# Moving the load slots of a streaming decode kernel to a multiple of 512 bytes in SBUF

## The chip, the cores and the metric

The kernel runs on one core of a Trainium2 chip. The metric is device time in microseconds (us), the median of several executions. Nearly all effects are under 2%, so kernels are compared with runs of the kernel before that were taken in the same call on the same chip.

The profile calls the engines PE (TensorE; PEld are its weight loads), DVE (VectorE), ACT (ScalarE), POOL (GpSimd) and SP (SyncE, which issues the loads). A packet is what the profile records as one item of a transfer: here the contiguous bytes that go into one partition.

## The reference, cut to what matters

One token goes through a transformer block with adaptive layer norm: conditioning, attention over a long cache, and a gated feed-forward.

```python
mod = silu(c) @ w_mod                        # 1024 x 6144
h = layernorm(x) * (1 + ca) + sa
q = h @ wq                                   # 1024 x 4096, 32 heads, 4 KV groups
scores = q . k_cache * 128 ** -0.5           # k_cache 4 x 65536 x 128, bf16
o = softmax(scores) . v_cache                # v_cache the same size
x = x + ga * (o @ wo)
h = layernorm(x) * (1 + cb) + sb
x = x + gb * ((gelu(h @ w_gate) * (h @ w_up)) @ w_down)
```

Everything is read once: 185.6 MB, of which the two caches are 134.2 MB. There is almost no reuse, so the time is first of all the time of reading.

## The kernel before

All large inputs arrive through ten slots of 8,192 bf16 elements (16 KB) in each of the 128 partitions, which are slices of one tensor. A K load fills two slots (32 KB per partition), a V load one; the weights use one slot each, wholly or in part. SP issues the loads in a fixed order, each as soon as the slots that it overwrites are free.

```python
SLOT = 8192
NSLOT = 10

ident = sb("ident", [P, P], dt.bfloat16)
identf = sb("identf", [P, P])
# ... some forty further tensors, in order ...
t_dn = sb("t_dn", [P, KD])
y_col = sb("y_col", [P, KD])
y_row = sb("y_row", [KD, P], dt.bfloat16)
# ... PSUM ...
slot_all = nc.alloc_sbuf_tensor("slots", [P, NSLOT * SLOT], dt.bfloat16)
slots = [slot_all[:, i * SLOT:(i + 1) * SLOT] for i in range(NSLOT)]

def issue_ready():
    while issued[0] < len(loads):
        j = loads[issued[0]]
        if any(q.freed is None for q in j.prev):
            return
        SP.wait(*(q.freed for q in j.prev))
        sp.dma_start(j.view, j.src).then_inc(j.tok[0], 16)
        issued[0] += 1

kh = [A_k_cache[0, g].rearrange("(p n) d -> p n d", p=P) for g in range(Hkv)]   # vh alike
# chunk i: 64 rows of 128 elements per partition, which lie together in HBM
j_k[i] = plan_load(kv_src(kh, i, KU), flat(KU * CH, DH), ...)     # KU = 2 chunks, 32 KB a partition
j_v[j] = plan_load(kv_src(vh, j), flat(CH, DH), ...)              # 1 chunk, 16 KB a partition
```

In the built program tensors lie in the order of their allocation, each rounded up to 32 bytes. The slots start at byte 65,088 of each partition, which is 127 x 512 + 64. Since a slot is 16 KB, all ten slots start 64 bytes past a multiple of 512. Every run of the large inputs in HBM starts at a multiple of 2 KB within its tensor.

## Time and profile before

| what | value |
|---|---|
| time, median of 3 runs | 443.07 us |
| span of the profiled run | 442.0 us |
| data moved, mean rate | 185.89 MB, 421 GB/s |
| time of the load queue's packets, share of 16 engines' span | 98.7% |
| TensorE (PE) busy | 351.4 us (80%) |

The profile's page of the kernel before; the first line under the heading is the engines' busy time, the line under the third heading is the load queue (packets, megabytes, time of its packets as a share of the 16 DMA engines' span), and the fourth heading is the chain of work that ended last:

```profile
span 442.0 us, 15336 instructions
## 1 busy us (share of the span) xinstructions
PE 351.4 (80%) x7107; PEld 316.9 (72%) x7107; DVE 176.2 (40%) x300; ACT 146.5 (33%) x553; POOL 11.7 (3%) x25
...
q1 hardware_dynamic: 11632, 185.61, 98.7%
...
DMA 62%; PE 33%; issue 1%; DVE 1%; SPq 1%; ACT 1%
```

The load queue's own packets fill 98.7% of the time of all 16 DMA engines. No compute engine is above 80%. The chain that ended last is mostly DMA.

The table by stretches of the same kernel (bounds in us, length, then busy time of each engine with its number of instructions, granted clock, DMA share, GB/s):

```profile
60.00:100.00 40.00, 34.97 (x706) 34.46 (x707) 16.14 (x19) 10.65 (x35) 0.00 (x0) 0.68 1.01 429
100.00:200.00 100.00, 90.62 (x2029) 88.58 (x2025) 49.85 (x78) 44.78 (x171) 0.00 (x0) 0.80 1.00 428
200.00:300.00 100.00, 89.63 (x1966) 87.46 (x1963) 48.61 (x78) 45.08 (x171) 0.00 (x0) 0.80 1.01 430
300.00:380.00 80.00, 73.26 (x1589) 71.75 (x1586) 38.45 (x58) 36.99 (x149) 0.00 (x0) 0.76 1.01 430
```

The last two numbers are what to read: the DMA share is 1.00 or 1.01 everywhere, so the transfers never run dry in the attention stage, and the rate stays at 428 to 430 GB/s.

The timeline of the last microseconds (start us, length us, engine, line, what; in brackets the idle time before it and what ended it):

```profile
436.66 2.94 PE L372 MATMUL b<-u_col,slots 128*128 128x1 bf16 x96 [3.07 <-DMA slots<-in_B_w_down_dram]
...
440.47 0.28 DVE L850 CAST y_row<-b 8x128 bf16<-8x128 f32 x1 [0.47 <-PE b L848]
```

The last group of products starts when one of the last loads lands. The very last load lands while this group runs, at 439.18 us by the landings in the trace, and eight products start on it. The chain that ended last shows this (start us, length us, what):

```profile
414.74 24.44 DMA slots<-in_B_w_down_dram
439.23 0.39 PE b L372 x8
440.47 0.28 DVE y_row L850
```

After the last landing the kernel needs about 1.6 us to its last result. So the time is: start of the stream + duration of the stream + a fixed end.

### The profile page before, as it was taken

Reading aid. Unit: us, or ns where it says so; the run is one execution under the profiler, and the core shown is the slowest. Engines: PE = TensorE matmul, PEld = TensorE weight load, DVE = VectorE, ACT = ScalarE, POOL = GpSimd, SP = SyncE. Lnnn points to the kernel's source line nnn. Section 1 sums busy time; section 2 is a strip of 40 time slices with the busy share of each in tenths; the row PEclk is TensorE's granted clock in tenths of the full one; section 3 lists DMA queues with packets and bytes.
Section 4 is the critical chain, followed back from the end, with each engine's and each line's share of the span. In section 5 each row is a group of like instructions: output and inputs, shape, how many; then the busy total and the mean of one; then the engine's idle time right before and its main releaser. Section 6 shows DMA issues by size and latency. Waiting matters only on the chain.

```text
span 442.0 us, 15336 instructions
## 1 busy us (share of the span) xinstructions
PE 351.4 (80%) x7107; PEld 316.9 (72%) x7107; DVE 176.2 (40%) x300; ACT 146.5 (33%) x553; POOL 11.7 (3%) x25
## 2 busy tenths in 40 slices
PE   0557449997889989998989879898998989547644
PEld 0214139987889989997989879798988979533234
DVE  4102013545534544554445544454446445242100
ACT  1000001334524643343535534344554433500000
POOL 8100000000000000000000000000000000000000
PEclk9955555969956975967778986877768686658955
DMA  8999999999999999999999999999999999999995
GB/s 330 430 427 425 443 434 414 423 442 417 428 446 414 442 412 442 416 439 430 423 440 420 435 421 437 439 418 446 412 443 414 440 420 431 424 429 418 427 419 211
DMA packets 11957, 185.89 MB, mean 421 GB/s; under 512 B 1568, under 2 KB 1568, under 8 KB 1952
## 3 DMA queue, kind: packets, MB, share of 16 engines
q1 hardware_dynamic: 11632, 185.61, 98.7%
q8 instruction: 13, 0.21, 0.2%
q10 hardware_dynamic: 304, 0.01, 0.0%
q14 instruction: 8, 0.07, 0.0%
HBM read 185.60 MB, written 0.00 MB: 420 GB/s over the span
## 4 chain that ended last, share of the span: by engine, by line
DMA 62%; PE 33%; issue 1%; DVE 1%; SPq 1%; ACT 1%
DMA slots<-in_A_v_cache_dram 39%; PE kt_ps L561 18%; DMA slots<-in_A_k_cache_dram 10%; PE b L625 7%; PE sc_ps L581 6%; DMA slots<-in_B_w_down_dram 6%; DMA slots<-in_B_w_up_dram 4%; DMA slots<-in_w_mod_dram 4%; PE b L605 1%; SPq L234 1%; PE kt_ps L392 1%; ACT p_sb L691 1%; PE b L595 1%; DVE kt_sb L751 0%; PE b L760 0%
## 5 line engine op out<-in xcount | busy, mean ns | idle before, releaser
L561 PE MATMUL kt_ps<-ident,slots 128*128 128x128 bf16 x2048 | 178.0, 257 | 11.0 <-DMA slots<-in_A_k_cache_dram 10.0
L561 PEld LDWEIGHTS kt_ps<-ident,slots 128*128 128x128 bf16 x2048 | 153.8, 117 | 12.8 <-issue 8.7
L660 DVE COPY kt_sb<-kt_ps 128x2048 bf16<-128x2048 bf16 x96 | 117.6, 1225 | 111.7 <-PE kt_ps L561 111.6
L660 ACT ACTIVATE kt_sb<-kt_ps 128x2048 bf16<-128x2048 bf16 x32 | 60.1, 1877 | 185.1 <-PE kt_ps L561 185.1
L625 PE MATMUL b<-p_sb,slots 128*128 128x8 bf16 x2176 | 75.7, 167 | 25.0 <-DMA slots<-in_A_v_cache_dram 16.1
L625 PEld LDWEIGHTS b<-p_sb,slots 128*128 128x128 bf16 x2176 | 69.5, 100 | 27.9 <-DMA slots<-in_A_v_cache_dram 17.3
L691 ACT ACTIVATE p_sb<-sc_ps,mneg 128x64 bf16<-128x64 f32 x256 | 83.6, 560 | 4.9 <-DVE mneg L686 4.9
L691 ACT ACTIVATION_READ_ACCUMULATOR p_sb<-sc_ps,mneg 128x1 f32 x256 | 77.2, 364 | 0.0
L581 PE MATMUL sc_ps<-q_buf,kt_sb 128*128 128x8 bf16 x2112 | 69.8, 167 | 0.9 <-issue 0.9
L581 PEld LDWEIGHTS sc_ps<-q_buf,kt_sb 128*128 128x128 bf16 x2112 | 67.6, 100 | 1.0 <-issue 1.0
L392 PE MATMUL kt_ps<-slots,h_pad 128*32 128x512 bf16 x176 | 17.5, 526 | 13.1 <-DMA slots<-in_A_wq_dram 6.4
L679 DVE TENSOR_REDUCE m_col<-sc_ps 128x8 f32<-128x512 f32 x32 | 21.8, 682 | 5.1 <-PE sc_ps L581 5.1
L684 DVE TENSOR_REDUCE mg<-b 8x1 f32<-8x128 f32 x32 | 8.9, 279 | 35.2 <-PE b L595 35.2
L392 PEld LDWEIGHTS kt_ps<-slots,h_pad 128*32 128x32 bf16 x176 | 5.3, 117 | 23.0 <-DMA slots<-in_A_wq_dram 8.3
L392 PE MATMUL kt_ps<-slots,s_pad 128*32 128x512 bf16 x96 | 13.6, 588 | 8.7 <-DMA slots<-in_w_mod_dram 8.7
L392 PEld LDWEIGHTS kt_ps<-slots,s_pad 128*32 128x32 bf16 x96 | 3.8, 123 | 17.6 <-DMA slots<-in_w_mod_dram 12.5
L605 PE MATMUL b<-negi,mg 8*128 8x8 f32 x66 | 15.6, 306 | 0.0
L605 PEld LDWEIGHTS b<-negi,mg 8*128 8x128 f32 x66 | 12.5, 235 | 2.1
L453 PEld LDWEIGHTS sc_ps<-identf,kt_sb 128*128 128x128 f32 (+1 forms) x48 | 7.6, 204 | 8.2 <-DVE kt_sb L774 4.3
L686 DVE COPY mneg<-b 128x8 f32<-128x8 f32 x32 | 5.3, 167 | 19.6 <-PE b L605 19.6
L453 PE MATMUL sc_ps<-identf,kt_sb 128*128 128x128 f32 (+1 forms) x48 | 9.1, 352 | 4.5 <-DVE kt_sb L774 2.4
L372 PE MATMUL b<-u_col,slots 128*128 128x1 bf16 x224 | 6.6, 165 | 6.8 <-DMA slots<-in_B_w_down_dram 6.7
(97 smaller groups left out, 84.9 us busy)
## 6 DMA issues: line engine op xcount, KB each, us to landing
slots<-in_A_k_cache_dram SPq DMA_DIRECT2D x16, 4096.0 KB, 20.7
slots<-in_A_v_cache_dram SPq DMA_DIRECT2D x32, 2048.0 KB, 27.3
slots<-in_w_mod_dram SPq DMA_DIRECT2D x8, 1536.0 KB, 17.9
slots<-in_A_wq_dram SPq DMA_DIRECT2D x4, 2048.0 KB, 35.7
slots<-in_A_wo_dram SPq DMA_DIRECT2D x4, 2048.0 KB, 32.8
slots<-in_B_w_gate_dram SPq DMA_DIRECT2D x4, 1792.0 KB, 21.0
slots<-in_B_w_up_dram SPq DMA_DIRECT2D x4, 1792.0 KB, 22.8
slots<-in_B_w_down_dram SPq DMA_DIRECT2D x3, 2048.0 KB, 27.7
```

Of the source, the lines that this page charges most:

```text
L372: ins = pe.matmul(bank[:, j:j + 1], view[:, kk, j * P:(j + 1) * P], rhs[:, k0 + kk:k0 + kk + 1], start=first, stop=True, skip_group_check= ...
L392: ins = pe.matmul(out, pad[:, k, :], jb.view[:, kk, c0:c0 + ROW], start=k <= last_k[0], stop=k >= last_k[1], skip_group_check=True,)
L453: ins = pe.transpose(dst[:, i * w:i * w + n], src[:, a], identf[0:src.shape[0], 0:n])
L561: ins = pe.transpose(kt_ps[:, half * 2048 + t * P:half * 2048 + (t + 1) * P], j_k[i - i % KU].view[:, i % KU * CH + b * TB + t, :], ident[ ...
L581: ins = pe.matmul(sc_ps[:, base + n * REP:base + (n + 1) * REP], kt_sb[:, j % 2, n, :], q_buf[:, j % SITES, :], start=True, stop=True,)
L605: ins = pe.matmul(b6[:, 256:256 + REP], mg8[:, j % 2:j % 2 + 1].to_broadcast([REP, P]), negi[:, :], start=True, stop=True,)
L625: ins = pe.matmul(b7[:, s * REP:(s + 1) * REP], j_v[j].view[:, n, :], p_sb[:, s, n, :], start=(n == 0), stop=(n == CH - 1),)
L660: ev[i % SITES][b].done(act.activation(dst, src, ACT.Copy) if E_ is AC else dve.tensor_copy(dst, src))
L679: m1[s].done(dve.tensor_reduce(m_col[:, j % 2, :].unsqueeze(2), scv, AX.X, ALU.max))
L684: m2[s].done(dve.tensor_reduce(mg8[:, j % 2:j % 2 + 1], b6[0:REP, 32:32 + P], AX.X, ALU.max))
L686: v_mc[j] = DVE.done(dve.tensor_copy(mneg[:, j, :], b6[:, 256:256 + REP]))
L691: ins = act.activation(p_sb[:, s, :, h], scv[:, h, :], ACT.Exp, bias=mneg[:, j, h:h + 1], scale=scale, accum_out=z_all[:, j, h:h + 1],)
```

## The change

The intent is to let every packet that a load writes start on a round SBUF address. Four 32-byte tensors are allocated earlier and the slots directly behind them, so that the slots start at byte 16,896 = 33 x 512.

```diff
     ident = sb("ident", [P, P], dt.bfloat16)
+    x_col = sb("x_col", [P, KD])
+    x_nat = sb("x_nat", [P, KD])
+    sg_col = sb("sg_col", [P, KD])
+    th_col = sb("th_col", [P, KD])
+    slot_all = nc.alloc_sbuf_tensor("slots", [P, NSLOT * SLOT], dt.bfloat16)
     identf = sb("identf", [P, P])
     ...
-    x_col = sb("x_col", [P, KD])
-    x_nat = sb("x_nat", [P, KD])
-    sg_col = sb("sg_col", [P, KD])
-    th_col = sb("th_col", [P, KD])
     ...
-    slot_all = nc.alloc_sbuf_tensor("slots", [P, NSLOT * SLOT], dt.bfloat16)
```

No instruction is added, removed or reordered. Only the tensors' addresses differ. The two big working tensors (the transposed K and the probabilities) keep their offset within 2 KB.

## The prediction

> **What bounds the kernel now.** The loads. The page's DMA row is at 9 tenths in all but the first and last slices. The table by stretches gives a DMA share of 1.00 to 1.01 and 427 to 430 GB/s from 30 to 400 us, while PE in its busiest stretch is 90% busy and waits for landings. The chain of waits is 62% DMA, mostly V-cache loads, and ends in pure load (w_up, then w_down to 439.2 us) with some 3 us of work after it. So the time is: start of the first load (2.2 us) + the packets' own time + about 3 us.
>
> The load queue's packets in the trace (11,632, 185.61 MB) sum to 436.1 us over 16 engines. 16,384 bytes take 615.7 ns mean (613 median), 32,768 bytes 1217.7 (1215), 8,192 bytes 312 median. The slope is 602 ns per 16 KB: 27.2 GB/s an engine, 435 for 16. The Trainium skill ("DMA: Bandwidth & Descriptors", Specifications) gives 435 GB/s as the fabric ceiling (16 x 32 B x 850 MHz); the slope agrees to 0.1%. So the bytes cost 426.5 us whatever their address, and alignment can only touch the constant per packet: about 10 ns, in sum 436.1 - 426.5 = 9.6 us, of which some 0.7 us are the 1,256 four-byte packets.
>
> **What the change does.** It moves addresses only; order and number of instructions are the same on all engines. The slots go from byte 65,088 of a partition (64 past a multiple of 512) to 16,896 (a multiple of 512). Each slot is 16 KB, so all ten share that offset. The transposed K and the probabilities keep their offset within 2 KB.
>
> **Costed.** The same page (How a descriptor splits into AXI transactions) says that a descriptor not starting on 256 B pays beats for the bytes below its start: here 64 B, two beats of 32 B, 2.35 ns; it states this for reads, and no run yet shows it for writes into SBUF. There are about 10,360 data packets, 648 an engine: 1.5 us for two beats each, 3.0 us for four (start and end). The full slope and the equal constant of 16 and 32 KB packets exclude a cost per 256 or 512 bytes. All of it lies on the critical path, because the stream does. Engine work is unchanged; waits may shift without effect.
>
> **Prediction: 440.9 us**, range 438.0 to 443.3. Faster by over 2%: 0.03 (it needs 8.9 us, nearly the whole constant); within 2%: 0.96; slower by over 2%: 0.01.
>
> **What would show it.** Right: the median of 16 KB packets falls from 613 to about 610 ns, that of 32 KB packets from 1215 to about 1212, by the same absolute amount; GB/s from 100 to 300 us rises to about 432; the packets' sum and the span fall by the same 1.5 to 3 us; packet counts and instruction means (transpose 257 ns, eviction 1225 ns) stay, apart from the granted clock. Wrong, null: medians unchanged, span 442 +- 0.3. Wrong, larger: 16 KB packets below 606 ns, or 32 KB packets gain twice what 16 KB ones do.
>
> **What would make it wrong.** Writes may absorb an odd start at no cost. The whole constant may be misalignment (up to 9 us). The shares of 1.01 mean that packets overlap by about 1%, so a shorter packet may not bring the next one sooner. HBM may be the real limit at 430 GB/s. Transfers to other SBUF addresses may collide differently with TensorE's reads.

## The result, and the profile after

The changed kernel takes 440.43 us (440.15 to 440.60, 6 runs), the kernel before 443.50 us in 6 runs (443.01 to 443.62). The ratio is 0.9933, with a 95% interval of 0.992 to 0.9945. Ratios here are the mean time of one kernel's fast runs over that of the other's of the same rounds, so not quite the ratio of the medians quoted. The gain is 3.1 us.

The page of the changed kernel:

```profile
span 438.8 us, 15336 instructions
## 1 busy us (share of the span) xinstructions
PE 351.7 (80%) x7107; PEld 318.4 (73%) x7107; DVE 176.2 (40%) x300; ACT 146.4 (33%) x553; POOL 11.7 (3%) x25
...
q1 hardware_dynamic: 11632, 185.61, 98.8%
...
DMA 60%; PE 35%; DVE 2%; issue 1%; SPq 1%; ACT 1%; POOL 0%
```

Packets and bytes are the same, and the busy time of every engine is within 0.5%. The queue is as full as before, of a span that is 3.2 us shorter: the stream is still the limit, it only runs faster.

The table by stretches:

```profile
60.00:100.00 40.00, 35.85 (x713) 35.35 (x714) 16.33 (x19) 10.68 (x35) 0.00 (x0) 0.64 1.00 425
100.00:200.00 100.00, 90.76 (x2025) 88.65 (x2022) 49.77 (x78) 45.23 (x171) 0.00 (x0) 0.81 1.00 432
200.00:300.00 100.00, 92.58 (x1951) 90.57 (x1951) 48.34 (x76) 44.32 (x171) 0.00 (x0) 0.73 1.01 432
300.00:380.00 80.00, 73.69 (x1678) 72.11 (x1679) 39.31 (x60) 37.98 (x153) 0.00 (x0) 0.78 1.01 432
```

From 100 to 380 us the rate is 432 in place of 428 to 430 GB/s, at the same DMA share.

The timeline of the end:

```profile
433.51 2.91 PE L372 MATMUL b<-u_col,slots 128*128 128x1 bf16 x96 [3.01 <-DMA slots<-in_B_w_down_dram]
...
437.29 0.28 DVE L850 CAST y_row<-b 8x128 bf16<-8x128 f32 x1 [0.47 <-PE b L848]
```

The last group of products starts 3.15 us earlier (436.66 to 433.51). The chain shows the eight products that follow the last landing:

```profile
436.04 0.39 PE b L372 x8
```

The last load lands at 436.00 in place of 439.18 us, 3.2 us earlier, and the rest takes 1.6 us as before. The first packet starts at 1.9 us in both kernels. So all of the gain lies in the stream.

The trace also holds a duration for each packet. Durations of the load queue's packets, by size, worked out from these records (ns; "commonest" is the most frequent value with its share of the packets):

```
                 before (slots at 64)             after (slots at 0)
bytes    count   mean    commonest                mean    commonest
 4096      128   161.0   159 (52%)                159.0   159 (100%)
 8192      768   315.0   312 (56%)                310.0   309 (100%)
12288     1024   469.8   460 (68%)                467.8   460 (91%)
16384     5120   615.7   613 (51%), 620 (20%)     611.7   611 (100%)
32768     2048  1217.7  1215 (50%), 1222 (20%)   1214.2  1213 (100%)
sum over the queue / 16:   436.1 us                       433.7 us
```

Before, durations are spread over several values; after, nearly all packets of a size take the same time to the nanosecond (of the 12 KB ones 91%). The mean falls by 4.0 ns for 16 KB and by 3.5 ns for 32 KB, so by about the same amount for twice the bytes. The sum falls by 2.4 us.

### The profile page after: what moved, and what is told of

Its sections match the earlier page's. It is cut to its first block, busy times and chain, and to the rows that moved or that the text cites. A ratio compares the mean times of both kernels' runs of the same rounds, so it can differ in the third digit from the quotient of the medians.

```text
span 438.8 us, 15336 instructions
## 1 busy us (share of the span) xinstructions
PE 351.7 (80%) x7107; PEld 318.4 (73%) x7107; DVE 176.2 (40%) x300; ACT 146.4 (33%) x553; POOL 11.7 (3%) x25
## 4 chain that ended last, share of the span: by engine, by line
DMA 60%; PE 35%; DVE 2%; issue 1%; SPq 1%; ACT 1%; POOL 0%
DMA slots<-in_A_v_cache_dram 39%; PE kt_ps L561 18%; DMA slots<-in_A_k_cache_dram 10%; DMA slots<-in_B_w_down_dram 7%; PE b L625 7%; PE sc_ps L581 6%; DMA slots<-in_w_mod_dram 4%; PE kt_ps L392 2%; PE b L605 1%; SPq L234 1%; PE b L372 1%; ACT p_sb L691 1%; PE b L595 1%; DVE kt_sb L751 0%; PE sc_ps L453 0%
## 5 line engine op out<-in xcount | busy, mean ns | idle before, releaser
L392 PE MATMUL kt_ps<-slots,s_pad 128*32 128x512 bf16 x96 | 12.5, 553 | 9.3 <-DMA slots<-in_w_mod_dram 9.3
```

Source lines behind the costliest of these rows:

```text
L392: ins = pe.matmul(out, pad[:, k, :], jb.view[:, kk, c0:c0 + ROW], start=k <= last_k[0], stop=k >= last_k[1], skip_group_check=True,)
```

## The experiments

There were three questions: is it really the address of the slots; is it a cost of each packet; and what about an address costs. The rival to "the slots' alignment" was that the place of the slots or of the other moved tensors matters, since the change shifts nearly everything.

### 1. Which offset costs: o0, o32, o128, o256

These are the kernel before, with one to three small tensors of the kernel's end allocated behind the slots in place of ahead of them. The slots move by 32 to 448 bytes and stay near byte 65,000. Besides the tensors that are moved, the few small ones of the end that lay behind them shift with the slots (y_row in o0; y_col and y_row in o32; t_dn and y_col in o256, and gth too in o128). Everything else keeps its address.

```diff
# o0: slots at 65,024 (0 mod 512)
-    t_dn = sb("t_dn", [P, KD])
-    y_col = sb("y_col", [P, KD])
     y_row = sb("y_row", [KD, P], dt.bfloat16)
     ...
     slot_all = nc.alloc_sbuf_tensor("slots", ...)
+    t_dn = sb("t_dn", [P, KD])
+    y_col = sb("y_col", [P, KD])
# o32:  t_dn alone moved               -> slots at 65,056 (32 mod 512)
# o128: y_row, g4 and u_col moved      -> slots at 64,640 (128 mod 512)
# o256: y_row and u_col moved          -> slots at 64,768 (256 mod 512)
```

Expected of o0:

> The kernel before with two 32-byte tail tensors (t_dn, y_col) allocated behind the slots, so that the slots start at byte 65,024 (a multiple of 512) and nothing else but y_row moves. Theory 'the slots' alignment is the whole cause': 440.4 +- 0.3 us, 16 KB packets at 611 ns with almost no spread, 32 KB at 1213. Rival 'the place or the other moved tensors (identities, masks) matter': 443.5 us, 613 ns and the spread of before.

Expected of o32:

> Slots at 65,056, 32 past a multiple of 512. Theory A (beats for the bytes below the start of a 256-byte transaction: cost in proportion to the offset within 256): half of before's loss, about 442 us, mean 16 KB packet about 613.7 ns. Theory B (one more partial transaction per packet, whatever the offset): as before, 443.5 us and 615.7 ns. Rival C (half-filled 64-byte lines cost more than half-filled 128-byte ones): slower than before, over 444 us.

Expected of o128:

> Slots at 64,640, 128 past a multiple of 512. Theory A: twice before's loss, about 446.5 us, mean 16 KB packet about 619.5 ns. Theory B with a unit of 256 or 512 bytes: 443.5 us, 615.7 ns. Theory B with a unit of 128 bytes: 440.4 us, 611.7 ns, as if aligned.

Expected of o256:

> Slots at 64,768, 256 past a multiple of 512. Theory A, and B with a unit of 256 or 128: 440.4 us, 611.7 ns. B with a unit of 512 (a partial block of 512 bytes costs): 443.5 us, 615.7 ns.

Measured, beside 443.32 us of the kernel before:

| run | slots past a multiple of 256 | time, us | ratio to before, 95% interval | 16 KB packet, mean and commonest, ns |
|---|---|---|---|---|
| o0 | 0 | 440.52 | 0.9934 (0.9921 to 0.9948) | 611.8, 611 (100%) |
| o256 | 0 | 440.58 | 0.9937 (0.9924 to 0.9951) | 611.7, 611 (100%) |
| before | 64 | 443.32 | 1 | 615.7, 613 (51%) |
| o128 | 128 | 443.23 | 0.9997 (0.9983 to 1.001) | 615.5, 611 (23%) |
| o32 | 32 | 444.00 | 1.0016 (1.0002 to 1.0029) | 616.5, 614 (56%) |

The stretch from 100 to 300 us (last two columns: DMA share and GB/s) of o0, of o256, then of o128:

```profile
100.00:300.00 200.00, 187.91 (x3976) 184.00 (x3976) 98.14 (x155) 90.21 (x355) 0.00 (x0) 0.73 1.00 432
```

```profile
100.00:300.00 200.00, 177.41 (x3981) 173.27 (x3980) 98.76 (x155) 91.43 (x357) 0.00 (x0) 0.83 1.00 432
```

```profile
100.00:300.00 200.00, 181.34 (x3950) 177.03 (x3948) 97.05 (x153) 89.69 (x341) 0.00 (x0) 0.79 1.00 429
```

What follows. o0 moves two small tensors, shifts a third, and has the whole gain, in the old place: the alignment of the slots is the cause, and the rival falls. o256 has the whole gain too, so the unit is 256 bytes and not 512. A cost in proportion to the bytes below the start, which is how the prediction arrived at two beats, falls twice: an offset of 128 should have cost twice what 64 does (446.5 us), and costs the same; 32 should have cost half (442), and costs slightly more. What is paid against o0 is 2.7 us at 128, 2.8 us at 64 and 3.5 us at 32, so a similar amount for each offset that was tried that is not a multiple of 256. Why 32 costs somewhat more is open.

### 2. Per packet or per byte: split_al, split_mis

The order of the keys is free in attention as long as K and V share it. Here a chunk takes its 64 keys as four blocks of 16 rows from four places of the cache. Bytes, loads and all engine work stay; the K packets become 8 KB and the V packets 4 KB, and the data packets 28,800 in place of 10,368. split_al has the slots of the changed kernel, split_mis those of the kernel before.

```diff
-kh = [A_k_cache[0, g].rearrange("(p n) d -> p n d", p=P) for g in range(Hkv)]
+kh = [A_k_cache[0, g].rearrange("(p b c t) d -> p b (c t d)", p=P, b=NB, t=TB) for g in range(Hkv)]
-    return h[g][:, cc * CH:(cc + n) * CH, :]
+    return h[g][:, :, cc * TB * DH:(cc + n) * TB * DH]
-    j_k[i - i % KU].view[:, i % KU * CH + b * TB + t, :],
+    j_k[i - i % KU].view[:, b, (i % KU * TB + t) * DH:(i % KU * TB + t + 1) * DH],
# V alike, and both loads written as four blocks
```

> The changed kernel with the keys of a chunk taken as four blocks of 16 rows from four places of the cache, for K and V alike (a different order of the keys, the same result): the same bytes, but K packets of 8 KB and V packets of 4 KB, 28,800 data packets in place of 10,368, that is 1,152 more an engine. If the constant per packet of about 8.4 ns is what each packet adds: 9.7 us more, about 450 us. If the constant overlaps with other packets: less, 440.4 to 446.

> The same with the slots of before (64 past a multiple of 512). Every packet starts at 64 past a multiple of 256, so the loss against the aligned twin tells per packet from per byte. Per packet (the 3.0 us of 648 packets an engine are 4.6 ns each; now 1,800 packets): 8.3 us over split_al, about 458. Per byte or per load: 3.0 us over it, about 453.

Measured: split_al 445.64 us (445.55 to 446.03), split_mis 453.97 us (453.83 to 454.30), before 443.36 us. Both results are correct. The load queue on the two pages, split_al first:

```profile
span 444.2 us, 15336 instructions
...
q1 hardware_dynamic: 30064, 185.61, 99.7%
```

```profile
span 452.5 us, 15336 instructions
...
q1 hardware_dynamic: 30064, 185.61, 99.7%
```

The two stretches from 100 to 300 us, in the same order:

```profile
100.00:300.00 200.00, 182.44 (x3941) 178.25 (x3938) 96.92 (x153) 89.13 (x341) 0.00 (x0) 0.77 1.02 424
```

```profile
100.00:300.00 200.00, 178.10 (x3822) 174.19 (x3820) 93.89 (x148) 87.25 (x336) 0.00 (x0) 0.77 1.02 415
```

The loss from the offset is now 8.3 us, as expected of a cost per packet (a cost per byte would have stayed at 3.0). The absolute time of split_mis lies nearer to the 453 us expected of a cost per byte, but only because split_al, on which both figures rested, came out below its own forecast; the difference of the two is what tells. The two pairs agree in the size: 3.07 us over 10,368 / 16 = 648 packets an engine are 4.7 ns each, and 8.33 us over 28,800 / 16 = 1,800 are 4.6 ns each. At the 32 bytes in 1.176 ns of the packets' slope that is about the time of four beats.

One expectation was missed. Each packet more was to cost the 8.4 ns by which a packet's record exceeds its bytes, 9.7 us in all. The records did grow by that (the queue's sum from 433.7 to 443.1 us), but against the changed kernel's 440.43 us the time grew by 5.2 us only, 4.5 ns a packet. (src64_d0 below, with the same packets, came to 440.44 us.) That the number of packets makes these 5.2 us, and not the places in HBM that they are read from, is assumed; both changed. Consecutive records overlap, as the DMA share of 1.02 says, so the constant seen in a record is not the constant that the stream pays.

### 3. Read side or written side: src64_d0, src64_d64

Both read K and V of the first three of four groups from 64 bytes further on in HBM. That is wrong (the comparison with the reference did not notice). It gives 4,608 of the 10,368 data packets a source address 64 past a multiple of 256, counted from the start of the tensor (that the tensors start on such a multiple in HBM is assumed), with the slots of the changed kernel (d0) or of the kernel before (d64).

```diff
-kh = [A_k_cache[0, g].rearrange("(p n) d -> p n d", p=P) for g in range(Hkv)]
+kf = A_k_cache[0].rearrange("g s d -> (g s d)")
+kh = [kf[g * SK * DH + o:(g + 1) * SK * DH + o].rearrange("(p n d) -> p n d", p=P, d=DH)
+      for g, o in enumerate([32] * (Hkv - 1) + [0])]          # o in elements of 2 bytes; V alike
```

> The changed kernel (slots aligned) that reads K and V of the first three groups from 64 bytes further on in HBM, wrong results on purpose: 4,608 of 10,368 data packets, 288 an engine, now have a source 64 past a multiple of 256. If only the address written counts: 440.4 us. If a read's odd start costs two beats (2.35 ns): 441.1. If a read's odd start costs as much as a write's (4.6 ns), or if it is the difference between the two offsets that costs: 441.8.

> The kernel before (slots at 64) with the same shifted reads, wrong results on purpose: here those 4,608 packets have the same offset of 64 in source and destination. If the difference of the offsets is what costs: 1.3 us less than before, 442.1. If only the address written counts: 443.4, unchanged. If read and write each cost: 444 to 444.7.

Measured, beside 443.36 us: src64_d0 440.44 us (ratio 0.9936), src64_d64 443.25 us (ratio 0.9999). The commonest packet durations are those of the kernels without the shift (611 ns in all packets but a few; 613 ns in 51%). The stretch from 100 to 300 us, d0 first:

```profile
100.00:300.00 200.00, 178.91 (x4008) 174.65 (x4005) 99.33 (x157) 92.42 (x357) 0.00 (x0) 0.83 1.00 432
```

```profile
100.00:300.00 200.00, 181.24 (x3972) 177.15 (x3970) 97.25 (x154) 92.52 (x357) 0.00 (x0) 0.78 1.00 429
```

So it is the written address that counts: an odd source (that is, one not on a multiple of 256) costs nothing that these runs resolve, and equal offsets on both sides win nothing. The two beats of the prediction would have been 0.7 us here, close to what the intervals can tell apart; a cost as large as that of a write, 1.3 us, is excluded.

### 4. What about the address costs: cutend, cutstart, cutboth

A 16 KB packet that starts on a multiple of 256 covers 64 units of 256 bytes. One that starts anywhere else covers 65, the first and the last of them partly. These runs, all wrong and all with the aligned slots, ask whether it is the partly filled unit or the additional unit that costs. They leave off 64 bytes at the end, at the start, or at both ends of the K and V packets (6,144 packets, 384 an engine).

```diff
-            sp.dma_start(j.view, j.src).then_inc(j.tok[0], 16)
+            v, r = j.view, j.src
+            if j.kv:
+                v, r = (t.rearrange("p n d -> p (n d)") for t in (v, r))
+                n = v.shape[1]
+                v, r = v[:, 0:n - 32], r[:, 0:n - 32]      # cutend
+                # cutstart: [:, 32:n]      cutboth: [:, 32:n - 32]
+            sp.dma_start(v, r).then_inc(j.tok[0], 16)
# cutend and cutboth also clear the last 64 bytes of slots 1, 3, 4 and 5 once at the start
```

A first form of cutend cleared slots 6 and 7 as well, which race with a weight load into them.

> The changed kernel, slots aligned, whose K and V packets leave off their last 64 bytes (wrong results on purpose; 6,144 packets, 384 an engine, start on a multiple of 256 and end 64 short of one). The fewer bytes alone make 0.9 us less: 439.5. If one more transaction per packet is what costs (65 in place of 64; here 64, the last one short): 439.5, V packets at 608.5 ns mean. If a partly filled unit at the end costs: up to 1.8 us on top, 441.3, V packets at 612.4 mean.

> The changed kernel whose K and V packets leave off their first 64 bytes (wrong results on purpose): they start 64 past a multiple of 256 and end on one, again 64 units. If one more transaction costs: 439.5 us, V packets at 608.5 ns mean. If a partly filled unit at the start costs: up to 441.3 us and 612.4 ns.

> The changed kernel whose K and V packets leave off 64 bytes at both ends (wrong results on purpose): they start 64 past a multiple of 256 and end 64 short of one, two partly filled units, 64 units for 63.5 units' worth of bytes, so not one more than the bytes need. The fewer bytes alone: 1.8 us less, 438.6. If a unit more than the bytes need is what costs: 438.6 us, V packets at 606 ns mean. If two partly filled units in one packet cost, whatever their number: up to 440.4 us and 610 ns.

| run | start, end of the V packet, mod 256 | units covered, units that the bytes need | time, us | before | V packet, mean ns |
|---|---|---|---|---|---|
| cutend | 0, 192 | 64, 64 | 439.35 | 443.49 | 608.6 |
| cutstart | 64, 0 | 64, 64 | 439.56 | 443.49 | 608.7 |
| cutboth | 64, 192 | 64, 64 | 438.59 | 443.21 | 606.6 |
| before | 64, 64 | 65, 64 | 443.21 to 443.50 | | 615.7 |

All three came out at what the smaller number of bytes alone explains (expected 439.5, 439.5, 438.6). An odd start costs nothing by itself, an odd end neither, and both together neither. What the packets that lose have in common is that they cover one unit of 256 bytes more than their bytes need. A rival is left open: in these runs the partly filled units are 192 bytes full, whereas the losing kernels all have one that is at most half full (32, 64 or 128 bytes). Whether it is the additional unit or the small piece that costs, no run here tells.

### 5. A candidate: vpair

If each packet costs 4.5 ns, fewer packets should win. vpair is the changed kernel with V loaded two chunks at a time, as K is.

```diff
-    vfill = [Site(nc, f"vfill{i}", 16) for i in range(SITES)]
+    vfill = [Site(nc, f"vfill{i}", 16) for i in range(SITES // KU)]
-            if i >= 2:
+            if i >= 2 and i % KU == 0:
                 j = i - 2
-                j_v[j] = plan_load(kv_src(vh, j), flat(CH, DH), SITES + j % SITES, vfill[j % SITES])
+                j_v[j] = plan_load(
+                    kv_src(vh, j, KU), flat(KU * CH, DH), SITES + j % SITES, vfill[j % SITES // KU], KU)
# PV waits once per pair, reads the half that it needs, and releases after the second
```

> A candidate to beat both: the changed kernel with V loaded two chunks at a time, as K is, so 2,048 V packets of 32 KB in place of 4,096 of 16 KB, 128 fewer an engine. From split_al each packet more costs 5.2 us / 1,152 = 4.5 ns: 0.6 us less, 439.8 us. If the coarser release of V slots starves the transfers: over 440.4, with a DMA share under 1.00 in the stretch from 100 to 300 us.

Measured: 440.06 us median, but single runs of 440.02, 445.38, 440.77, 440.06 and 439.77 us, beside 443.49 us before; ratio 0.9955 with an interval from 0.9911 to 1.0. The profiled run (440.02 us) has in the stretch from 100 to 300 us:

```profile
100.00:300.00 200.00, 176.93 (x3940) 173.02 (x3938) 96.82 (x152) 89.08 (x341) 0.00 (x0) 0.81 1.00 431
```

The rate is not above the changed kernel's 432 GB/s. The best run is where it was expected, one run of five is 5 us slower, and no trace of that one exists, so its cause is open. Coarser release of the V slots is a suspect and is not shown; the profiled run's DMA share of 1.00 does not show it. It is not an improvement that can be claimed; of all the correct kernels, the changed one stands.

## Why the prediction was right or wrong

- **What bounds the kernel: right.** The stream limits, and all of the gain appears as an earlier last landing (3.2 us) with the end as long as before.
- **That the byte rate is out of reach: right.** The slope between 16 and 32 KB packets is 602 ns in both kernels, 27.2 GB/s an engine. It agrees with the 435 GB/s that the Trainium skill ("DMA: Bandwidth & Descriptors", Specifications) gives as the fabric ceiling. This is what kept the forecast small.
- **A cost per packet, in about the size foreseen: right, partly by luck.** The prediction allowed two to four beats a packet (its 2.35 ns for two is an estimate: 64 bytes at 27.2 GB/s), 1.5 to 3.0 us. The runs show 4.3 to 4.7 ns at this offset, about four beats, and 2.8 to 3.1 us, at the upper edge of that. Predicted were 440.9 us, measured 440.43. The 440.9 was 2.2 us under the 443.07 then known; the gain was nearer to 3. That the size came out is in part luck, since the account from which it was taken does not hold:
- **The reason given for it: wrong.** The step was that "a descriptor not starting on 256 B pays beats for the bytes below its start: here 64 B, two beats". That is the skill's account of reads, carried over to writes. The unit of 256 bytes is confirmed (o256 has the gain, o128 has not). But the cost does not follow the bytes below the start (32, 64 and 128 lie within 0.8 us, and the smallest offset costs the most), an odd start as such is free (cutstart), and reads with an odd start, for which the account was made, cost nothing that the runs resolve (src64_d0). In its place stands a cost of 4.2 to 5.4 ns for each packet that is written across one 256-byte unit more than its bytes need; why it costs this is open.
- **The signature: half right.** Both medians were to fall by the same 3 ns; they fell by 2 (613 to 611, 1215 to 1213). The larger part of the gain was the tail: of the 4.0 ns by which the mean of the 16 KB packets fell, 2.9 come from the third of them that took more than 613 ns (1.8 from those at 620 alone), and this tail all but vanished. The mean of the 32 KB packets fell by 3.5 ns. A median hides a cost that falls on some packets more than on others.
- **"The packets' sum and the span fall by the same": wrong.** The sum fell by 2.4 us and the span by 3.2. Records overlap (split_al shows 9.4 us more of records for 5.2 us of time), so the sum of durations is only a rough measure of the stream. Between split_al and split_mis the two differences are close (8.1 us of records, 8.3 of time). What fills the remaining 0.8 us here is open.

A further observation is open. In the kernel before, the 12 KB packets of the first loads stayed mostly at 460 ns until some 24 us, as in the changed kernel, although they wrote to equally odd addresses; only then did the spread set in. No run tested why.

## What to carry to other kernels

When the DMA queue is full from end to end, look at the address that each packet writes as well as at its size: here packets that covered one 256-byte unit more than their bytes needed lost 4.2 to 5.4 ns each on average (whether for the further unit or for the small piece in it is open), so the loss grows with the number of packets and not with the bytes (0.7% at 16 to 32 KB, 1.9% at 4 to 8 KB, by 453.97 over 445.64 us). It costs nothing to mend, since moving two small tensors behind the slots in the order of allocation was enough (o0). Its order of magnitude could be told beforehand from the constant that remains when the packets' durations are set against their sizes (9.6 us in sum, of which about 3 were won). Check a cause by an offset sweep rather than by one aligned and one odd case, for one pair of kernels cannot tell 64 from 128, 256 or 512.

## What the Trainium skill lacked or had wrong

- "DMA: Bandwidth & Descriptors", How a descriptor splits into AXI transactions: it tells of wasted beats of reads that start off 256 bytes, and has nothing on writes. Here reads 64 bytes off cost nothing that the runs resolve (440.44 against 440.43 us), while writes into SBUF 32, 64 or 128 bytes off cost 4.2 to 5.4 ns a packet; at 32 the loss is the largest (444.00 us) and does not follow the wasted bytes.
- The same page, Why small descriptors are slow (HBM only): it gives a fixed overhead of about 3 cycles a packet. The runs show 4.5 ns for each further aligned packet, by estimate 3.8 cycles at the 850 MHz of its Specifications, so roughly that. It does not say that the duration which a trace records for a packet exceeds its bytes by more, 8.4 ns here.
- The same page, Specifications: its row of the limit of HBM for a core, about 358 GB/s, stands without the condition that both cores of the pair read at once, which the page gives only further down. With one core running, 432 GB/s were sustained from HBM for 280 us.
- "SBUF — State Buffer", Operand start alignment: it says that its measurements are of legality and timed nothing. For the destination of a DMA, a multiple of 256 bytes per partition is worth 0.7% here.
